# An attention kernel whose exponentials write eight fixed buffers in turn, with the order between them and the maxima declared away

## The chip, the cores and the metric

The kernel runs on one core of a Trainium2 chip. The metric is the device time of one execution in microseconds; the time before is the median of three runs, 921.76 us. The core has five engines with queues of their own: TensorE (PE, whose weight loads are listed as PEld), VectorE (DVE), ScalarE (ACT), GpSimd (POOL) and SyncE (SP, which here starts the DMAs). They meet only at semaphores: an instruction may wait until another engine's counter has reached a value, and its queue stands still behind it until then.

## The reference

Two attentions over the same x (2048 x 448, 16 heads of 28), mixed by a gate for each row:

```python
x = A_x
g = _sigmoid((x * gate_w).sum(-1, keepdims=True))
a = _A_ref(x, A_wqkv, A_wo)
b = _B_ref(x, B_wqkv, B_wo)
return g * a + (1 - g) * b
...
scores = jnp.einsum("bhqd,bhkd->bhqk", q, k) * (Dh ** -0.5)
p = _softmax(scores, axis=-1)
o = jnp.einsum("bhqk,bhkd->bhqd", p, v)
```

A is local: each position looks at eight positions, two apart, back from itself. B, of which the last three lines are the core, is full softmax attention. The output is float32.

## The kernel before, in words

The kernel has three stages. Up to some 260 us it projects x to the queries, keys and values of both attentions. Each number is split there into a high and a low part of a faster matmul format, and a product is summed from three products of parts. From 261 us on runs the main loop of B, and behind it, from about 845 us, the output projection.

The main loop has 256 steps: 16 units u (four groups g of four heads, by four blocks b of 512 queries), and in each unit 16 blocks kt of 128 keys. The softmax of a unit needs the maximum of each row ahead of its exponentials, so there are two passes. The first pass computes plain scores in high parts only (`s1_mm`, L142, 1024 matmuls in all) and takes maxima over 512 keys (`s1_max`, L146). The first 320 of these tiles are done among the projections; the other 704 are spread over the main loop, three to a step, for units that come later. So 235 steps carry first-pass work and the last 21 don't. The second pass computes the scores of the present unit (`scores`, L959: three matmuls a head, the terms QH·KH, QL·KH and QH·KL, with the negative maximum riding in two extra rows of QH), then the exponential (L962), and one step later the product with the values (`do_av`, L925).

The order of every engine's queue is the order of the code (`manual_schedule`); the framework only places the semaphore waits. A step's order on PE is written out as a list of tokens:

```python
WITH = "10 20 s0 11 21 30 00 12 22 31 01 s1 s2 32 02".split()
```

A token of two digits is a score matmul: the first digit is the head in the step's rotation, the second the term. `s0`, `s1` and `s2` are the first-pass matmuls. Heads 1 and 2 fill the two banks of the PSUM pair `one`; behind token 22 ACT turns both into probabilities with one exponential, the first of the step. Heads 3 and 0 fill the pair `mine`; behind 02 comes the second. Token s0 fills the single bank T1, read by a maximum of 128 x 512 (the T1 maximum). s1 and s2 fill the third pair, `other`, read by one maximum of 128 x 1024 (the pair maximum). After each step `mine` and `other` change places. So tokens 30 and 00 write banks that the pair maximum of the step before has read, and s1 and s2 write banks that the second exponential of the step before has read. Last on PE in each step come the four AV matmuls of the step before (each has two records in the trace).

An exponential writes a probability tile of 128 x 1024 from the pool `pp`, which has eight slots; each exponential asks for a new tile, `pair("P")`. The AV matmuls read it a step later.

Besides this, DVE and POOL compute attention A during the steps up to about 760 us: POOL multiplies queries by shifted keys (L599), folds 40 of the 64 products to half their length (L604), and DVE sums them in 176 small sums (L609); POOL then multiplies by the values and adds up (L649, L654). A list with costs and due steps sets behind which step each of these instructions stands. DVE has the T1 maximum, the pair maximum and then the small sums in each step; ACT has the two exponentials and now and then a copy.

Where an instruction needs more than one semaphore, the framework puts the further waits into separate EVENT_SEMAPHORE instructions ahead of it on its queue; a view of the trace by line lists them under DVEq and ACTq.

Of the kernel before, what the change touches and what calls it, by code (L numbers as in the profile page):

```python
# [10 lines left out]
AF = mybir.ActivationFunctionType  # L11
ALU = mybir.AluOpType
X = mybir.AxisListType.X
# [6 lines left out]
SCALE = DH ** -0.5  # L20
NU = NG * NB
NMX = 192
# [3 lines left out]
def gated_mix_kernel(ctx: ExitStack, tc: tile.TileContext, xT, xn, gw, wA, wB, woAB, out):  # L26
    nc = tc.nc
# [45 lines left out]
    MX = cp.tile([128, NMX], F32, name="MX")  # L73
# [10 lines left out]
    def pair(name):  # L84
        return pp.tile([128, 2, 512], F32, tag="P", name=name)
# [50 lines left out]
    def s1_mm(n, bank, half=False):  # L136
        u, i = divmod(n, 64)
        qs, kc, h = i // 16, i // 4 % 4, i % 4
        if i == 0 and u + 1 < NU:
            load_qhi(u + 1)  # L140
        r = slice(64 * (h // 2), 64 * (h // 2) + 64) if half else slice(32 * h, 32 * h + DH)
        nc.tensor.matmul(bank, qhis[u][h % 2][r, 128 * qs:128 * qs + 128],  # L142
                         KH[u // NB % 3][r, 512 * kc:512 * kc + 512], start=True, stop=True)

    def s1_max(n, k, bank):
        nc.vector.tensor_reduce(MX[:, n % NMX:n % NMX + k], bank, axis=X, op=ALU.max)  # L146
        if n // 64 != (n + k) // 64:
            finished.append(n // 64)
        s1c[0] = n + k
# [53 lines left out]
    with tc.tile_pool(name="xp", bufs=1) as xp, tc.tile_pool(name="wp", bufs=2) as wp:  # L203
# [208 lines left out]
        for kt in range(3):  # L412
            if kt < 2:
                nc.vector.tensor_copy(xh[0][:, kt, :], r[:, kt, :])
            nc.vector.tensor_tensor(out=xl[0][:, kt, :], in0=r[:, kt, :], in1=xh[0][:, kt, :].bitcast(F32),
                                    op=ALU.subtract)
        nc.vector.tensor_tensor(out=tail[64:128], in0=t[64:128], in1=tail[64:128].bitcast(F32), op=ALU.subtract)
        nc.vector.tensor_tensor(out=wl0[:, 3, 0:256], in0=wt0[:, 0:256], in1=wh0[:, 3, 0:256].bitcast(F32),
                                op=ALU.subtract)
# [27 lines left out]
        for n, t in enumerate(tiles):  # L447
# [4 lines left out]
            for w in splits:  # L452
                i, k = (n - splits[w][0]) * splits[w][1], splits[w][1]
# [42 lines left out]
            if n == 64:  # L496
                gate = []
                for sgn, dst in ((-1.0, g_t), (1.0, omg)):
                    e = sp.tile([128, NJ], F32, name="ez")
# [174 lines left out]
    for c in range(8):  # L674
# [20 lines left out]
        n = 0  # L695
# [240 lines left out]
    def scores(u, kt, cur):  # L936
        g = u // NB
        n = s1c[0]
        k = min(3, s1e - n)
        qh, ql = Qs[u]  # L940
        ks = slice(128 * kt, 128 * kt + 128)
        one, mine, other = ring
        ring[:] = (one, other, mine) if k else (other, one, mine)
        bank = {"1": one[:, 0, :], "2": one[:, 1, :], "3": mine[:, 0, :], "0": mine[:, 1, :],
                "s0": T1, "s1": other[:, 0, :], "s2": other[:, 1, :]}
        for tok in WITH if k else ALONE:
            if tok[0] == "s":
                i = int(tok[1])
                if i < k:
                    s1_mm(n + i, bank[tok])  # L950
                if i == 0:
                    s1_max(n, 1, T1)
                elif i == 2 and k > 1:
                    s1_max(n + 1, k - 1, other[:, 0:k - 1, :])
                continue
            a, t = tok[0], int(tok[1])
            h = (int(a) + n) % 4
            r = slice(32 * h, 32 * h + (DH + 2 if t == 0 else DH))
            nc.tensor.matmul(bank[a], (KH[g % 3], KH[g % 3], KL[g % 2])[t][r, ks], (qh, ql, qh)[t][r, :], start=(t == 0), stop=(t == 2))  # L959
            if t == 2 and a in "20":  # L960
                p = pair("P")
                nc.scalar.activation(p, one if a == "2" else mine, AF.Exp, scale=SCALE)  # L962
                cur[(h + 3) % 4], cur[h] = p[:, 0, :], p[:, 1, :]
                yield len(cur)

    for u in range(NU):
        g, b = divmod(u, NB)
        for kt in range(NJ):
# [12 lines left out]
            for a in scores(u, kt, cur):  # L981
                if a == 2:
                    run("mid", st)
# [66 lines left out]
```

## Time and profile before

| | |
|---|---|
| times of three runs | 921.76, 920.22, 921.76 us |
| span of the profiled execution | 921.0 us |
| main loop, steps with first-pass work | 261 to 794 us |
| main loop, steps without it | 794 to about 845 us |
| DVE busy in 350 to 700 us | 331.19 us |
| POOL busy in 350 to 700 us | 342.62 us |
| granted clock, 261 to 794 us | 1.00 |

A row of the groups reads: line, engine, operation, what it writes and reads with partitions x elements, how often, then busy time and mean duration in ns, then the idle time of the engine just before them and what ended it. A row of the order in time reads: start and length in us, engine, line, operation, and in brackets the idle time before. Neighbouring instructions of one group are merged in one row, so "x2" is two of them in one stretch. The ends of matmuls are modelled.

### The profile page before, as it was taken

The page shows a single profiled execution, that of the slowest core. Times are in us where ns is not written, and L with a number is a line of the kernel's source. Part 1 is how long each engine was busy: PE and PEld are TensorE (multiplying, and loading weights), DVE is VectorE, ACT ScalarE, POOL GpSimd, SP SyncE. Part 2 cuts the span into 40 slices and gives each one's busy share as a digit, 9 for nine tenths or more (in the row PEclk, how much of TensorE's full clock was granted, in tenths as well). Part 3 has the DMA queues.
Part 4 walks back from the last instruction along what each step waited for, and adds up shares of the span by engine and source line. Part 5 has one row for each costly group of instructions (what it writes and reads, how often), then busy time and mean ns, then how long its engine had stood idle before and what let it go on. Part 6 is the DMA issues. An engine that isn't in the chain of part 4 may idle for free.

```text
span 921.0 us, 21402 instructions
## 1 busy us (share of the span) xinstructions
PE 911.3 (99%) x8390; PEld 547.3 (59%) x8390; DVE 731.6 (79%) x975; ACT 649.8 (71%) x797; POOL 624.0 (68%) x488
## 2 busy tenths in 40 slices
PE   8999999999999999999999999999999999999998
PEld 6799999998944444444444444444444444335997
DVE  6488999998979999999999999999998888501221
ACT  6456434343378888888888888888989889996221
POOL 2389846464469799999999999999994851300100
PEclk9999999999999999999999999999999999999999
DMA  9877503559462342235135232431312123441572
GB/s 264 276 247 193 158 12 82 142 132 97 116 241 64 101 121 51 84 105 129 41 94 157 83 102 61 132 84 26 106 47 53 33 50 100 135 132 51 158 218 87
DMA packets 103966, 105.11 MB, mean 114 GB/s; under 512 B 64136, under 2 KB 73736, under 8 KB 103080
## 3 DMA queue, kind: packets, MB, share of 16 engines
q1 hardware_dynamic: 103720, 103.47, 41.5%
q8 instruction: 66, 1.08, 0.5%
q10 hardware_dynamic: 144, 0.26, 0.1%
q14 instruction: 36, 0.29, 0.1%
HBM read 62.72 MB, written 40.96 MB: 113 GB/s over the span
## 4 chain that ended last, share of the span: by engine, by line
PE 96%; DMA 2%; DVE 1%; ACT 1%; issue 0%; SPq 0%; ACTq 0%; DVEq 0%
PE T L959 31%; PE av L925 27%; PE r L295 15%; PE T L803 7%; PE r L290 6%; PE r L142 4%; PE T L142 4%; DMA V<-in_xT 1%; PE T L781 1%; DMA KH<-qk_hi 0%; DMA qk_hi<-qkh 0%; ACT P L962 0%; DVE xl L212 0%; SPq L99 0%; DVE MX L159 0%
## 5 line engine op out<-in xcount | busy, mean ns | idle before, releaser
L962 ACT ACTIVATE P<-T 128x1024 f32<-128x1024 f32 x512 | 497.0, 1024 | 66.0 <-PE T L959 64.9
L146 DVE TENSOR_REDUCE MX<-T 128x1 f32<-128x512 f32 x470 | 443.4, 954 | 39.2 <-PE T L959 16.4
L925 PE MATMUL av<-P,V 128*32 128x512 f32 x2048 | 272.7, 605 | 0.4 <-ACT osb L821 0.4
L959 PEld LDWEIGHTS T<-QH,KH 30*128 30x128 f32 x1024 | 92.5, 181 | 238.4 <-ACT P L962 197.5
L959 PE MATMUL T<-QH,KH 30*128 30x512 f32 x1024 | 222.9, 492 | 0.2 <-ACT P L962 0.2
L142 PE MATMUL T<-KH,QP 28*128 28x512 f32 x704 | 222.6, 463 | 0.1
L159 DVE TENSOR_REDUCE MX<-r 128x2 f32<-128x1024 f32 x160 | 192.1, 1222 | 27.1 <-PE r L142 23.4
L959 PE MATMUL T<-QH,KL 28*128 28x512 f32 x1024 | 190.8, 391 | 0.0
L959 PE MATMUL T<-QL,KH 28*128 28x512 f32 x1024 | 190.2, 392 | 0.0
L599 POOL TENSOR_TENSOR prod<-qt,kt 128x896 f32<-128x896 f32 x64 | 135.1, 2115 | 4.8 <-DMA kt<-a_scr 4.8
L358 ACT ACTIVATE raw<-r 128x896 f32<-128x896 f32 (+1 forms) x64 | 58.9, 921 | 99.4 <-PE r L295 93.7
L654 POOL TENSOR_TENSOR oat<-oat,prod 128x896 f32<-128x896 f32 x56 | 118.2, 2110 | 2.4
L142 PEld LDWEIGHTS T<-KH,QP 28*128 28x128 f32 x704 | 86.0, 181 | 23.2 <-ACT P L962 10.2
L359 POOL TENSOR_TENSOR ast<-raw 128x448 f32<-128x448 f32 x48 | 55.5, 1155 | 60.3 <-ACT raw L358 50.6
L649 POOL TENSOR_TENSOR prod<-vt,L 128x896 f32<-128x896 f32 x56 | 95.4, 1704 | 0.6
L959 PEld LDWEIGHTS T<-QH,KL 28*128 28x128 f32 x1024 | 93.5, 183 | 0.7
L959 PEld LDWEIGHTS T<-QL,KH 28*128 28x128 f32 x1024 | 93.4, 184 | 0.0
L925 PEld LDWEIGHTS av<-P,V 128*32 128x32 f32 x2048 | 40.3, 108 | 79.9 <-issue 66.8
L295 PE MATMUL r<-wh,xh 64*128 64x448 f32 (+1 forms) x512 | 82.8, 363 | 0.3 <-ACT raw L358 0.3
L142 PE MATMUL r<-KH,QP 64*128 64x512 f32 x320 | 80.5, 394 | 2.0 <-DMA KH<-qk_hi 0.8
L295 PE MATMUL r<-wh,xl 64*128 64x448 f32 (+1 forms) x384 | 70.4, 364 | 0.0
L295 PEld LDWEIGHTS r<-wh,xh 64*128 64x128 f32 x512 | 63.2, 185 | 1.5 <-ACT raw L358 0.6
(101 smaller groups left out, 1049.9 us busy)
## 6 DMA issues: line engine op xcount, KB each, us to landing
a_scr<-ast SPq DMA_DIRECT2D x24, 448.0 KB
qk_hi<-qkh SPq DMA_DIRECT2D x24, 256.0 KB
qk_lo<-qkh SPq DMA_DIRECT2D x24, 256.0 KB
rbc<-rs SPq DMA_DIRECT2D x64, 64.0 KB
QP<-qk_hi SPq DMA_DIRECT2D x64, 56.0 KB
KL<-qk_lo SPq DMA_DIRECT2D x16, 224.0 KB
QH<-qk_hi SPq DMA_DIRECT2D x64, 56.0 KB
QL<-qk_lo SPq DMA_DIRECT2D x64, 56.0 KB
```

Of the source, the lines that this page charges most:

```text
L142: nc.tensor.matmul(bank, qhis[u][h % 2][r, 128 * qs:128 * qs + 128], KH[u // NB % 3][r, 512 * kc:512 * kc + 512], start=True, stop=True)
L146: nc.vector.tensor_reduce(MX[:, n % NMX:n % NMX + k], bank, axis=X, op=ALU.max)
L159: nc.vector.tensor_reduce(m, PM[k], axis=X, op=ALU.max)
L295: nc.tensor.matmul(bank[:, 0:cols], x, ws[c][rows, k, 0:cols], start=first, stop=last)
L358: nc.scalar.activation(raw[:, :, 0:cols], PJ[n % 2][:, :, 0:cols], AF.Copy)
L599: nc.gpsimd.tensor_tensor(out=p, in0=qt[c], in1=kvt["k", c % 2][:, HALO - DIL * w:HALO - DIL * w + NJ, :], op=ALU.mult)
L649: nc.gpsimd.tensor_tensor(out=dst.rearrange("p j (h d) -> p j h d", d=DH), in0=kvt["v", c % 2][:, HALO - DIL * w:HALO - DIL * w + NJ, :].r ...
L654: nc.gpsimd.tensor_tensor(out=oat[c], in0=oat[c], in1=oat[c, w], op=ALU.add)
L803: writes(bank, nc.tensor.matmul(bank[:, :D], src, wo[c][:, k, :], start=(first and k == ks[0] and i == 0), stop=(last and k == ks[-1] and ...
L925: nc.tensor.matmul(av[32 * h:32 * h + 32, :], V[:, kt, 4 * g + h, :], tiles_[h], start=(kt == 0), stop=(kt == NJ - 1), skip_group_check=True)
L959: nc.tensor.matmul(bank[a], (KH[g % 3], KH[g % 3], KL[g % 2])[t][r, ks], (qh, ql, qh)[t][r, :], start=(t == 0), stop=(t == 2))
L962: nc.scalar.activation(p, one if a == "2" else mine, AF.Exp, scale=SCALE)
```

## The change

Two things change, both in the main loop. The first eight exponentials take a probability tile from the pool and keep it in a list; every later one writes the tile of eight exponentials before instead of asking for a new one. And edges are declared to the framework as needing no wait: from a maximum to the last eight exponentials; from an exponential to the one that wrote its buffer before; and from an exponential to the last four maxima. The reasons given in the code are that PE waited for the one named and the instruction at hand waits for PE. The waits for PE stay. No instruction that computes is added, removed or moved; the 176 small sums and the 40 folds are as they were.

```diff
+    exps, maxs, probs = [], [], []
+
     def s1_max(n, k, bank):
-        nc.vector.tensor_reduce(MX[:, n % NMX:n % NMX + k], bank, axis=X, op=ALU.max)
+        i = nc.vector.tensor_reduce(MX[:, n % NMX:n % NMX + k], bank, axis=X, op=ALU.max)
+        for e in exps[-8:]:
+            tc.declare_no_dep(i.ins, e, reason="PE waited for it and the maximum waits for PE")
+        maxs.append(i.ins)
         if n // 64 != (n + k) // 64:
             finished.append(n // 64)
         s1c[0] = n + k
...
             if t == 2 and a in "20":
-                p = pair("P")
-                nc.scalar.activation(p, one if a == "2" else mine, AF.Exp, scale=SCALE)
+                if len(exps) < 8:
+                    probs.append(pair("P"))
+                p = probs[len(exps) % 8]
+                e = nc.scalar.activation(p, one if a == "2" else mine, AF.Exp, scale=SCALE).ins
+                for o in exps[-8:-7]:
+                    tc.declare_no_dep(e, o, query=mybir.DependencyQuery.ANY_SYNC,
+                                      reason="PE has read what it wrote, and this one waits for PE")
+                for o in maxs[-4:]:
+                    tc.declare_no_dep(e, o, reason="PE waited for it and the exponential waits for PE")
+                exps.append(e)
                 cur[(h + 3) % 4], cur[h] = p[:, 0, :], p[:, 1, :]
                 yield len(cur)
```

## The prediction

> **What bounds the kernel now.** I read the page first, then the busy time by stretch, the groups by form and the waits inside the main loop, and last a few steps in order of time.
>
> ```profile
> span 921.0 us, 21402 instructions
> PE 911.3 (99%) x8390; PEld 547.3 (59%) x8390; DVE 731.6 (79%) x975; ACT 649.8 (71%) x797; POOL 624.0 (68%) x488
> ...
> PE 96%; DMA 2%; DVE 1%; ACT 1%; issue 0%; SPq 0%; ACTq 0%; DVEq 0%
> ```
> ```profile
> 261.00:794.00 533.00, 532.78 (x5354) 220.51 (x5346) 496.22 (x717) 469.14 (x530) 462.51 (x323) 1.00 0.34 91
> 350.00:700.00 350.00, 349.78 (x3516) 144.73 (x3512) 331.19 (x499) 307.12 (x347) 342.62 (x229) 1.00 0.33 86
> ```
>
> Columns of the second view: stretch, length, busy time of PE, PEld, DVE, ACT, POOL, granted clock, DMA share, GB/s. Everything the diff touches runs between 261 and 794 us, the steps that mix second-pass scores with first-pass maxima. PE looks full there, the chain of work that ended last is 96% PE and the clock is whole, so removing waits on ACT and DVE would seem to buy nothing. But matmuls on different row groups overlap, and a busy PE need not be at its peak. DVE is busy for 496.2/533 = 93%, ACT for 88%.
>
> ```profile
> L962 ACT ACTIVATE P<-T 128x1024 f32<-128x1024 f32 x466 | 452.5, 1024 | 63.9 <-PE T L959 62.8
> L146 DVE TENSOR_REDUCE MX<-T 128x2 f32<-128x1024 f32 x233 | 285.0, 1223 | 19.8 <-PE T L959 11.1 <-PE T L142 0.2
> L925 PE MATMUL av<-P,V 128*32 128x512 f32 x1864 | 248.2, 605 | 0.0
> L609 DVE TENSOR_REDUCE L<-prod 128x8 f32<-128x224 f32 x96 | 33.7, 371 | 0.0
> ```
>
> Eight AV records make a step: 1864/8 = 233 steps in 533 us, 2.29 us each. Now three of them.
>
> ```profile
> 500.83 0.50 PE L959 MATMUL T<-QH,KH 30*128 30x512 f32 x2
> ...
> 501.40 2.01 DVE L146 TENSOR_REDUCE MX<-T 128x1 f32<-128x512 f32 x2
> ...
> 501.64 0.42 PE L142 MATMUL T<-KH,QP 28*128 28x512 f32 x2
> ...
> 501.90 1.94 ACT L962 ACTIVATE P<-T 128x1024 f32<-128x1024 f32 x2 [0.39 <-PE T L959]
> 502.13 1.06 PE L925 MATMUL av<-P,V 128*32 128x512 f32 x8
> 503.13 0.49 PE L959 MATMUL T<-QH,KH 30*128 30x512 f32 x2
> ...
> 503.47 0.50 PE L959 MATMUL T<-QH,KH 30*128 30x512 f32 x2
> ...
> 503.70 0.39 PE L959 MATMUL T<-QH,KL 28*128 28x512 f32 x2
> ...
> 504.20 1.94 ACT L962 ACTIVATE P<-T 128x1024 f32<-128x1024 f32 x2
> 504.37 1.06 PE L925 MATMUL av<-P,V 128*32 128x512 f32 x8
> 505.36 0.50 PE L959 MATMUL T<-QH,KH 30*128 30x512 f32 x2
> ...
> 506.19 0.49 PE L142 MATMUL T<-KH,QP 28*128 28x512 f32 x2
> ...
> 506.80 1.23 DVE L146 TENSOR_REDUCE MX<-T 128x2 f32<-128x1024 f32 x1 [0.16 <-PE T L959]
> ...
> 508.06 0.64 DVE L609 TENSOR_REDUCE L<-prod 128x16 f32<-128x224 f32 x2
> 508.08 0.50 PE L959 MATMUL T<-QH,KH 30*128 30x512 f32 x2
> ...
> 508.62 1.81 DVE L146 TENSOR_REDUCE MX<-T 128x1 f32<-128x512 f32 x2
> ...
> 509.97 0.50 PE L959 MATMUL T<-QH,KH 30*128 30x512 f32 x2
> ...
> 510.48 0.50 PE L959 MATMUL T<-QH,KH 30*128 30x512 f32 x2
> ...
> 512.36 0.50 PE L959 MATMUL T<-QH,KH 30*128 30x512 f32 x2
> ```
>
> Columns: start and length in us. A step opens with QH,KH of tokens 10 and 20 (500.83, 503.13, 505.36). The opening waits for no exponential: it comes 1.00 us after the AV group's start at 502.13 and 0.99 after that at 504.37, although the first exponential of the pair (1.02 us each) ended 0.21 us before the one opening and 0.14 before the other. It is PE's own pace.
>
> The second QH,KH pair, tokens 30 and 00, is different. At 503.47 it follows the end of the pair maximum (501.40 + 2.01 = 503.41) by 0.06; at 508.08 it follows 506.80 + 1.23 = 508.03 by 0.05; at 510.48 it follows 508.62 + 1.81 = 510.43 by 0.05. That maximum reads the bank pair into which these matmuls write. So 30/00 come 0.34 us after the opening at 503.13 but 0.51 after that at 509.97, and the next opening comes 1.89, 1.89 and 1.88 us after the three: the delay goes through to the step. PE, busy or not, runs at the pace of loops through DVE and ACT. Three kinds show here.
>
> *Loop A*, two steps: opening 500.83, first-pass matmuls s1/s2 501.64, pair maximum until 503.41, 30/00 503.47, opening 505.36. 4.53 us, 2.27 a step, one pair maximum that waited for PE.
> *Loop B*, three steps: opening 503.13, exponentials 504.20 to 506.14, s1/s2 0.05 later at 506.19 (they write what the second exponential read), pair maximum 506.80 to 508.03, 30/00 508.08, opening 509.97. 6.84 us, 2.28 a step, one exponential and one pair maximum that waited for PE.
> *Chained DVE*: where DVE has no gap (508.06 local sums, 508.62 both maxima, until 510.43), a loop gains one step in which nothing waits for PE: B becomes 503.13 to 512.36, 9.23 us over four, 2.31 a step.
>
> **The change, part by part.** *Fixed buffers.* The pool already holds eight slots and nothing else takes them in this loop, so the same eight buffers come round in the same order: no memory, copy or DMA is added, and the price is nothing. The three lists are made in Python and issue nothing.
>
> *Waits removed.*
>
> ```profile
> L962 ACT ACTIVATE P<-T x175: 1017/1024/1049, 499.6 to 699.2; 128x1024 f32<-128x1024 f32 x175
> L962 ACTq EVENT_SEMAPHORE  x173: 17/17/17, 501.8 to 699.5; - x173
> L146 DVE TENSOR_REDUCE MX<-T x176: 624/952/1227, 499.4 to 699.6; 128x1 f32<-128x512 f32 x88, 128x2 f32<-128x1024 f32 x88
> L146 DVEq EVENT_SEMAPHORE  x87: 21/21/21, 502.1 to 699.5; - x87
> ```
>
> Almost every exponential has a separate wait ahead of it, and of the maxima one kind does: 87 waits for 88 pair maxima. An instruction holds one wait itself; a second becomes an instruction of its own. The declared edges leave each with PE alone, so the separate instructions should go: some 233 on DVE and 466 to 512 on ACT. Most of them stand ahead of an instruction that queues behind its own engine anyway (the second exponential; the maxima in the 1.81 us pair at 508.62, shorter than 0.69 + 1.23 on their own) and are worth nothing, as the running instruction covers them. Where the engine idles until PE is done, the wait is on the path. Its price is how much later the work starts than with PE's wait inside the instruction:
>
> ```profile
> L146 DVEq EVENT_SEMAPHORE  x1: 21/21/21, 548.0 to 548.0; - x1
> 548.02 1.23 DVE L146 TENSOR_REDUCE MX<-T 128x2 f32<-128x1024 f32 x1 [0.19 <-PE T L959]
> L962 ACTq EVENT_SEMAPHORE  x2: 17/17/17, 568.2 to 568.3; - x2
> 568.31 1.02 ACT L962 ACTIVATE P<-T 128x1024 f32<-128x1024 f32 x1 [0.38 <-PE T L959]
> 516.87 0.49 PE L142 MATMUL T<-KH,QP 28*128 28x512 f32 x1
> 517.44 0.69 DVE L146 TENSOR_REDUCE MX<-T 128x1 f32<-128x512 f32 x1 [0.17 <-PE T L142]
> ```
>
> A wait shown at 548.0 ended no earlier than 547.95, and its maximum began at 548.02: at most 0.07 between. One shown at 568.2 was no later than 568.25, its exponential began at 568.31: at least 0.06. From below: a T1 maximum, whose only wait is in the instruction, starts 517.44 − (516.87 + 0.49) = 0.08 us after the modelled end of its matmul, the pair maximum 506.80 − (506.19 + 0.49) = 0.12 after, the exponential 504.20 − (503.70 + 0.39) = 0.11 after: 0.03 to 0.04. So the bounds are 0.03 and 0.07. I take 0.065 for DVE and 0.06 for ACT, because the wait's own record is nearer to the thing than a modelled end.
>
> By the Trainium skill, "VectorE: DVE Perf Modes", section "The DRAIN you can't avoid", a semaphore after each of a chain of DVE operations cost nothing extra over one at the end. That would make this edit worth zero; the rows agree where DVE queues behind itself, and not where it idles until PE.
>
> *The sum.* Loop A saves 0.065 in two steps, 0.033 a step; loop B 0.125 in three, 0.042; with a chained step these become 0.022 and 0.031. Over 233 steps: 7.6, 9.7, 5.1 and 7.3 us. Following the releases back from the last such step to the first, as above, I count 69 loops, 51 of them through an exponential: 69 × 0.065 + 51 × 0.06 = 7.5 us. That is the most this chain can give, since others almost as long take over as it shrinks. I take the middle between it and the lowest loop: (7.5 + 5.1)/2 = 6.3 us. With prices of 0.03 for both it would be 3.6 on the same chain, with 0.07 for both 8.4.
>
> *Late next.* PE's own pace: the step opened at 503.13 lasted 2.23 us, still under 2.29 − 0.03 = 2.26. And POOL: 342.6 of 350 us busy leaves 7.4 us, 0.048 a step over 153 steps, above the 0.027 I use.
>
> Span: 921.0 − 6.3 = 914.7. The median shown is 0.8 above this span; 921.8 − 6.3 = 915.5 us.
>
> **The rivals.** *POOL takes over.* If its 7.4 us are gaps it cannot close, the 153 steps keep their pace and only 80 gain, 80 × 0.027 to 0.042 = 2.2 to 3.4 us: 918.4 to 919.6. For it: the 98%. Against: the local sums, which need POOL's products, show 0.0 us of idle before them.
>
> *Nothing to gain.* The waits are free, or the framework puts others in their place (the exponential's wait for the AV matmuls that read its buffer, say, which is PE's too and should fold into the one kept): 921.8. Against the first: the 0.06 above.
>
> *The loops go altogether*, all steps at 2.23 us: 233 × 0.06 = 14 us, 908. It needs DVE to stop queueing at 93% busy.
>
> *Slower.* Telling the framework less makes other instructions wait for themselves. The dear place is PE ahead of its AV group: if fixed buffers make it wait for the exponentials separately, at 0.06 (ACT's price) on the engine that closes every loop, 233 steps cost 14.0 us, less 6.3 is 7.7: 929.5. From 6.3/0.06 = 105 such waits on, the kernel is slower.
>
> ```profile
> PEld T L959 <- ACT P L962: 194.8, 232, 1.1
> PEld av L925 <- issue: 65.8, 219, 0.4
> ```
>
> Against it: the opening weight loads already carry a wait for the exponential, 232 times; the AV group comes later on the same queue, and its idle time shows no release by ACT P now.
>
> **How the numbers follow.** A difference under 0.2% (1.84 us) can't be told from no change. Forecast, with any mix of the loops (5.1 to 9.7 saved, 912 to 916.7): 0.60. POOL or another chain keeps part of it (1.9 to 5.1 saved): 0.16. Loops go further than 9.7: 0.07. Nothing: 0.11. Slower: 0.06. Faster is 0.60 + 0.16 + 0.07 = 0.83. The range 910.5 to 920.3 takes in both prices of the wait and leaves out nothing gained, slower, and the far part of the large gain, 0.20 in all.
>
> **What would show it.** The separate waits of L962 and L146 fall from about one per exponential and per pair maximum to a handful. An exponential that idled starts about 0.05 us, not 0.11, after its matmul's modelled end; a pair maximum 0.06, not 0.12. 30/00 still follow the pair maximum by 0.05, now nearer to the opening, and the stretch of 233 steps shrinks from 533 to about 527 us. Before 261 us and after 794 nothing moves. A shorter lag with the same step would say the loops are not the bound; a wait of POOL's ahead of the local sums would be the first rival; idle before the AV loads released by ACT P, the last.

## The result, and the profile after

The changed kernel takes 913.08 us (912.09 to 914.14), the kernel before 921.76. The ratio is 0.9913, 95% interval 0.9896 to 0.9929: between 6.5 and 9.6 us faster, where 6.3 was forecast. In a later set of runs the same pair gave 0.9920 (0.9907 to 0.9932).

The page after, its busy line and its chain:

```profile
span 910.4 us, 20673 instructions
PE 901.8 (99%) x8390; PEld 545.7 (60%) x8390; DVE 730.6 (80%) x975; ACT 649.1 (71%) x797; POOL 623.1 (68%) x488
...
PE 72%; POOL 20%; DMA 4%; SPq 1%; issue 1%; DVE 1%; ACT 1%; POOLq 0%; ACTq 0%
```

There are 21402 − 20673 = 729 instructions fewer, and no computing one among them: the counts behind the five engines are as before. What is gone shows in the views by line, 500 to 700 us, which before listed 173 and 87 separate waits:

```profile
L969 ACT ACTIVATE P<-T x177: 1003/1023/1046, 499.8 to 699.5; 128x1024 f32<-128x1024 f32 x177
L148 DVE TENSOR_REDUCE MX<-T x178: 630/950/1227, 499.4 to 699.9; 128x1 f32<-128x512 f32 x89, 128x2 f32<-128x1024 f32 x89
```

Neither line lists an EVENT_SEMAPHORE now. (L969 is L962 of before, L148 is L146, L964 is L959, L930 is L925.) The groups of the main loop:

```profile
L969 ACT ACTIVATE P<-T 128x1024 f32<-128x1024 f32 x465 | 451.7, 1025 | 56.5 <-PE T L964 55.4
L148 DVE TENSOR_REDUCE MX<-T 128x2 f32<-128x1024 f32 x232 | 283.6, 1222 | 8.0 <-PE T L964 1.3 <-PE T L142 0.2
L148 DVE TENSOR_REDUCE MX<-T 128x1 f32<-128x512 f32 x233 | 160.1, 687 | 22.3 <-PE T L142 13.1 <-PE T L964 6.8
```

The durations are the same; the idle time ahead of the pair maxima fell from 19.8 to 8.0 us, that ahead of the exponentials from 63.9 to 56.5. That ahead of the T1 maxima rose from 16.7 to 22.3. Some rows in order of time show the lags:

```profile
501.12 0.50 PE L964 MATMUL T<-QH,KH 30*128 30x512 f32 x2
...
501.49 0.50 PE L964 MATMUL T<-QH,KH 30*128 30x512 f32 x2
...
501.69 0.39 PE L964 MATMUL T<-QH,KL 28*128 28x512 f32 x2
...
502.02 1.81 DVE L148 TENSOR_REDUCE MX<-T 128x1 f32<-128x512 f32 x2
...
502.13 1.94 ACT L969 ACTIVATE P<-T 128x1024 f32<-128x1024 f32 x2 [0.38 <-PE T L964]
...
503.37 0.50 PE L964 MATMUL T<-QH,KH 30*128 30x512 f32 x2
```
```profile
558.33 0.50 PE L142 MATMUL T<-KH,QP 28*128 28x512 f32 x2
558.87 1.23 DVE L148 TENSOR_REDUCE MX<-T 128x2 f32<-128x1024 f32 x1
```

The exponential starts 502.13 − (501.69 + 0.39) = 0.05 us after the modelled end of its matmul, where 0.11 was read before. The pair maximum starts 558.87 − (558.33 + 0.50) = 0.04 after, where it was 0.12. The rows are typical: over the steps with first-pass work, the median lag of the first exponential fell from 0.104 to 0.043 us, that of the pair maximum from 0.113 to 0.044. Tokens 30/00 come 0.37 us after this opening, and the next opening 1.88 us after them, as before.

To see where the time came from, each execution is cut at three records of the AV matmuls: the first, the first of the 234th group and the first of the last (256th) group. That gives four parts: what is ahead of the loop, the 233 steps, the 22 up to the last AV group, and the tail.

| profiled execution | ahead | 233 steps | last steps | tail | span |
|---|---|---|---|---|---|
| before | 261.5 | 533.9 | 47.0 | 78.5 | 921.0 |
| before, again | 262.0 | 534.1 | 47.0 | 78.6 | 921.6 |
| after | 258.2 | 527.2 | 46.4 | 78.6 | 910.4 |
| after, again | 259.3 | 527.2 | 46.5 | 78.6 | 911.4 |

The part ahead holds no edited line, and its differences look like chance: it varies between 258.2 and 262.0 us over the kernels of this study, whether they have the change or not. The 233 steps repeat to 0.1 us. So the change is worth 533.94 − 527.23 = 6.7 us there and 0.5 us in the last steps, 7.2 together; the 8.7 between the two medians probably holds some of that chance besides, and 7.2 lies within both intervals.

### The profile page after: what moved, and what is told of

Same layout as the page of the kernel before. It is cut to its first block, busy times and chain, and to the rows that moved or that the text cites. A ratio compares the mean times of both kernels' runs of the same rounds, so it can differ in the third digit from the quotient of the medians.

```text
span 910.4 us, 20673 instructions
## 1 busy us (share of the span) xinstructions
PE 901.8 (99%) x8390; PEld 545.7 (60%) x8390; DVE 730.6 (80%) x975; ACT 649.1 (71%) x797; POOL 623.1 (68%) x488
## 3 DMA queue, kind: packets, MB, share of 16 engines
q8 instruction: 66, 1.08, 0.5%
## 4 chain that ended last, share of the span: by engine, by line
PE 72%; POOL 20%; DMA 4%; SPq 1%; issue 1%; DVE 1%; ACT 1%; POOLq 0%; ACTq 0%
PE T L964 19%; PE av L930 17%; PE r L300 15%; PE T L808 8%; PE r L295 6%; POOL oat L659 6%; POOL prod L604 5%; POOL prod L654 5%; PE r L142 4%; PE T L142 3%; DMA V<-in_xT 1%; POOL prod L609 1%; DMA oa_scr<-oat 1%; POOL on L855 1%; SPq L99 1%
## 5 line engine op out<-in xcount | busy, mean ns | idle before, releaser
L969 ACT ACTIVATE P<-T 128x1024 f32<-128x1024 f32 x512 | 496.9, 1025 | 58.2 <-PE T L964 56.3
L148 DVE TENSOR_REDUCE MX<-T 128x1 f32<-128x512 f32 x470 | 441.5, 954 | 33.1 <-PE T L142 15.7
L930 PE MATMUL av<-P,V 128*32 128x512 f32 x2048 | 272.8, 605 | 0.4 <-ACT osb L826 0.4
L964 PEld LDWEIGHTS T<-QH,KH 30*128 30x128 f32 x1024 | 92.6, 182 | 231.5 <-ACT P L969 199.0
L142 PE MATMUL T<-KH,QP 28*128 28x512 f32 x704 | 220.3, 456 | 0.1
L964 PE MATMUL T<-QH,KH 30*128 30x512 f32 x1024 | 213.0, 490 | 1.8 <-ACT P L969 1.1
L964 PE MATMUL T<-QH,KL 28*128 28x512 f32 x1024 | 187.0, 395 | 0.0
L964 PE MATMUL T<-QL,KH 28*128 28x512 f32 x1024 | 185.1, 393 | 0.0
L964 PEld LDWEIGHTS T<-QL,KH 28*128 28x128 f32 x1024 | 94.1, 185 | 0.0
L964 PEld LDWEIGHTS T<-QH,KL 28*128 28x128 f32 x1024 | 93.6, 183 | 0.6
L930 PEld LDWEIGHTS av<-P,V 128*32 128x32 f32 x2048 | 40.5, 108 | 78.0 <-issue 65.1
```

What stands on the lines that cost most here:

```text
L148: i = nc.vector.tensor_reduce(MX[:, n % NMX:n % NMX + k], bank, axis=X, op=ALU.max)
L930: nc.tensor.matmul(av[32 * h:32 * h + 32, :], V[:, kt, 4 * g + h, :], tiles_[h], start=(kt == 0), stop=(kt == NJ - 1), skip_group_check=True)
L969: e = nc.scalar.activation(p, one if a == "2" else mine, AF.Exp, scale=SCALE).ins
```

## The experiments

Each was compared with runs of the kernel before on the same chip. "Steps" are the 233 steps of its profile, cut as above. The diffs are against the changed kernel.

**The parts of the change, one at a time.** First the unchanged kernel for its stages:

> The kernel before once more, unchanged, for its stages. The 233 steps took 534 us before and 527 after, and the projections ahead of them 261.5 and 258.2 us, though the diff doesn't touch them. If those 3.4 us are chance, this run may show projections anywhere near 258 to 262 us, with 233 steps of 534 us again. If the change itself shortened the projections, they take 261 to 262 us here and 258 in every kernel that has the change.

Steps 534.1 us; ahead of them 262.0. Then only the maxima:

```diff
-                if len(exps) < 8:
-                    probs.append(pair("P"))
-                p = probs[len(exps) % 8]
+                p = pair("P")
...
-                for o in exps[-8:-7]:
...
-                for o in maxs[-4:]:
```

> Only the maxima lose their waits for exponentials; the exponentials are as before, with new buffers from the pool. Loops theory: each of the 69 loops has one pair maximum that waits for PE, 69 x 0.065 = 4.5 us at most, some 3.8 expected; 233 steps of 530 us, about 918 us. Rival (ACT alone carries the gain, the maxima queue behind DVE anyway): 921.8 us, 233 steps of 534.

917.2 us, ratio 0.9958 (0.9942 to 0.9974), steps 529.5: 4.5 less. Only the exponentials:

```diff
-        for e in exps[-8:]:
-            tc.declare_no_dep(i.ins, e, reason="PE waited for it and the maximum waits for PE")
```

> Only the exponentials change (fixed buffers, no waits for maxima and for themselves); the maxima keep their separate wait. Loops theory: 51 of the 69 loops pass through an exponential that waits for PE, 51 x 0.06 = 3.1 us at most, some 2.6 expected; 233 steps of 531.4 us, about 919.2 us. Rival (ACT alone): the whole gain, about 913 us. Rival (maxima alone): 921.8 us.

917.1 us, 0.9952 (0.9939 to 0.9964), steps 530.3: 3.6 less, and 46.5 in the last steps, where the maxima alone gave 47.3. Then the buffers, with no declared edge:

> The eight fixed buffers with no edge declared away: every separate wait is there as before. Loops theory: no difference, 921.8 us within 0.2%, 233 steps of 534 us. Rival (the buffers themselves save something, for instance in what the pool's release costs): up to the 8.7 us of the change, 913 us.

921.7 us, 0.9999 (0.9990 to 1.0008), steps 534.2. The buffers by themselves do nothing. The views by line, 500 to 700 us, show which wait each variant kept; first the one with the maxima alone, then the one with the exponentials alone:

```profile
L967 ACTq EVENT_SEMAPHORE  x175: 17/17/411, 500.7 to 698.4; - x175
```
```profile
L148 DVEq EVENT_SEMAPHORE  x88: 21/21/21, 500.5 to 698.8; - x88
```

Both kinds of wait pay, and neither rival that gave all to one of them holds.

**Which of the exponentials' waits.** Two complements, both with fixed buffers and the maxima left alone: one loses only the wait for itself, the other only the waits for maxima.

```diff
-                for o in maxs[-4:]:
-                    tc.declare_no_dep(e, o, reason="PE waited for it and the exponential waits for PE")
```

> As in the run with the exponentials alone, but only the wait for themselves is declared away, so the second exponential of each step keeps a separate wait for a maximum and the first one has none. Loops theory: the second one queues behind the first anyway, so its separate wait is free: the same 917.1 us as with both declared (233 steps 530.3 us). Rival (every separate wait costs): half the gain, about 919.3 us.

917.6 us, 0.9951 (0.9939 to 0.9964), steps 530.1. The view by line of this kernel, 500 to 700 us:

```profile
L967 ACT ACTIVATE P<-T x176: 1015/1023/1060, 499.7 to 699.3; 128x1024 f32<-128x1024 f32 x176
L967 ACTq EVENT_SEMAPHORE  x83: 17/17/17, 503.3 to 699.3; - x83
```

83 waits for 176 exponentials: half of them kept one, and the gain is the same as with none.

```diff
-                for o in exps[-8:-7]:
-                    tc.declare_no_dep(e, o, query=mybir.DependencyQuery.ANY_SYNC,
-                                      reason="PE has read what it wrote, and this one waits for PE")
```

> The complement: fixed buffers, only the exponentials' waits for maxima declared away, the wait for themselves kept, so that PE's wait stands in a separate instruction ahead of every exponential. Loops theory: nothing, 921.7 us within 0.2%, 233 steps 534 us. Rival (every separate wait costs): some 2 us faster.

921.9 us, 0.9997 (0.9989 to 1.0006), steps 534.1. The records of the trace say which semaphore stands where. In the kernel before and in this one, an exponential that finds ACT idle has the wait for PE in the separate instruction and the wait for ACT itself in its own; with the wait for itself gone it holds PE's wait alone, and nearly all separate waits that are left belong to exponentials that queue behind ACT and wait for DVE. So the exponentials' gain comes from the first of each step, where the wait for PE moved into the instruction; the second queues behind it and its separate wait costs nothing. Two of the three sets of edges do the work: those of the maxima, and that of an exponential to the writer of its buffer. (No run has these two sets and not the third.)

**Is POOL the next bound?** After the change the page puts 20% of its chain on POOL.

```diff
-            nc.gpsimd.tensor_tensor(out=oat[c], in0=oat[c], in1=oat[c, w], op=ALU.add)
+            if w % 2 == 0:
+                nc.gpsimd.tensor_tensor(out=oat[c], in0=oat[c], in1=oat[c, w], op=ALU.add)
```

> The changed kernel with 32 of POOL's 56 additions of local attention left out (those of odd shifts; the local attention is then incomplete): 32 x 2.11 = 68 us less on POOL. Loops theory: POOL is not the bound, 913.1 us within 0.2%, 233 steps 527 us. Rival (POOL is the new bound after the change, its share of the chain being 20% on the page): several us faster, 233 steps under 524 us.

913.7 us, 0.9907 (0.9893 to 0.9920): no different from the change in its time, in which 261.6 us ahead of the loop hide it, but the steps took 525.3 us, 1.9 less than with the change. The trace says where. The changed kernel at a unit's end, in order of time:

```profile
614.38 1.31 POOL L855 TENSOR_TENSOR on<-osb,rbc 128x512 f32<-128x512 f32 x1
...
615.73 0.63 ACT L859 ACTIVATE onhi<-on 128x512 fp32r<-128x512 f32 x1 [1.08 <-POOL on L855]
...
616.27 1.92 ACT L969 ACTIVATE P<-T 128x1024 f32<-128x1024 f32 x2
...
617.33 0.50 PE L964 MATMUL T<-QH,KH 30*128 30x512 f32 x2 [1.11 <-ACT P L969]
```

And the kernel before at the same place:

```profile
620.33 1.29 POOL L850 TENSOR_TENSOR on<-osb,rbc 128x512 f32<-128x512 f32 x1
...
622.86 0.63 ACT L854 ACTIVATE onhi<-on 128x512 fp32r<-128x512 f32 x1
623.38 1.94 ACT L962 ACTIVATE P<-T 128x1024 f32<-128x1024 f32 x2
```

Before, POOL ended its product at 621.62 and ACT reached the copy that needs it 1.24 us later. With shorter steps ACT reaches it first, waits 1.08 us at the head of its queue, the exponentials behind it are late, and now the opening does wait for an exponential. The waits of PE in the loop of the changed kernel:

```profile
PE T L964 <- ACT P L969: 1.1, 1, 1.1
PE T L964 <- DMA QH<-nm: 0.6, 1, 0.6
```

They sum to 1.7 us, at two openings of new units; before it was 0.2 us, and with less on POOL the view is empty. The second row is the other place, and there POOL seems to act through SyncE: SyncE's queue stood 8.7 us for another product of POOL (L840), and behind it stand the loads for the next unit, on the last of which the opening waited. POOL is a bound in two places of 233, not in the loop at large.

**Are the chained steps the rest?** The changed kernel with short small sums:

```diff
-        nc.vector.tensor_reduce(..., prods[c, w][:, r], axis=X, op=ALU.add)
+        nc.vector.tensor_reduce(..., prods[c, w][:, r, 0:2], axis=X, op=ALU.add)
```

> The changed kernel with each of the 176 small sums reading 2 elements of a row in place of 14 or 28 (the local scores are then incomplete): each some 0.25 us shorter, 44 us less on DVE. Loops theory: the chained steps vanish, what is left are loops A at (4.53 - 0.065)/2 = 2.23 and B at (6.84 - 0.125)/3 = 2.24 us a step: 233 steps of 520 to 522 us against 527, some 6 us faster, 907 us. Rival (PE's own pace now sets the step): no change, 913 us.

914.4 us, 0.9917 (0.9902 to 0.9933), steps 526.9: a miss. The sums were indeed short, by the groups of DVE in its main loop:

```profile
L148 DVE TENSOR_REDUCE MX<-T 128x1 f32<-128x512 f32 x466 | 444.1, 956 | 52.5 <-PE T L142 26.2 <-PE T L964 9.3
L614 DVE TENSOR_REDUCE L<-prod 128x16 f32<-128x32 f32 (+1 forms) x176 | 24.6, 163 | 0.0
```

DVE gained 37 us and spent it waiting for PE. Part of the expected gain went into the same two openings, where PE now lost more:

```profile
PE T L964 <- ACT P L969: 1.6, 1, 1.6
PE T L964 <- DMA QH<-nm: 1.4, 1, 1.4
```

Without them the steps are 523.9 against 525.5 for the change, 1.6 us for the 37.

The releases can be followed back through this trace as in the prediction, a matmul being counted as held where it starts within 0.08 us of the end that it waits for. Of 70 loops, 46 are then of kind B without chained DVE, at 2.240 us a step: the 2.24 that was expected. Of the rest, 13 take four steps and have one of ACT's copies in the queue with the exponentials, at 2.26 to 2.27 us a step but for the one with the late opening. Chained DVE stands in 6 loops, where the changed kernel has it in 35 of 64. So the chained steps did go, but most of the chained loops had taken only 2.25 to 2.26 us a step in the changed kernel, little above B's 2.24, and there was little to gain.

Two more runs tried ACT's copies (the first with the short sums as well):

```diff
-        nc.scalar.activation(t, av, AF.Copy)
+        if u < NU - 1:
+            nc.vector.tensor_copy(t, av)
...
-        nc.scalar.activation(fin["hi"], fin["on"], AF.Copy)
+        if u < NU - 1:
+            nc.vector.tensor_copy(fin["hi"], fin["on"])
...
```

> The kernel with short small sums (local scores incomplete, as there) and with ACT's two larger copies of each unit, 0.6 us each, moved to DVE, which has room there. That kernel kept 2.26 us a step although the loops A and B, with the durations measured in it, give 2.22 to 2.24. Theory (ACT's copies stretch the loops that pass through the exponentials): steps of 2.24 us or less, 233 steps about 521 us against 527, time about 908 us. Rival (something else, PE's own pace for one): 527 us again, 914 us.

921.0 us, 0.9997 (0.9988 to 1.0006), steps 534.8.

> The same move of ACT's two copies to DVE in the changed kernel with its sums whole. DVE gains 1.2 us in 16 steps and ACT loses it. If ACT's copies are on the loops more often than DVE has a queue: some us faster, 908 to 912 us. If DVE's queue pays as much as ACT saves: 913 us or slower.

926.8 us, 1.0055 (1.0039 to 1.0071), steps 538.1. Both are slower than their counterparts by 8 and 11 us of steps. They don't show what the copies cost on ACT, because the move is no exchange of equals: the copy that rounds took 0.63 us on ACT and, in the first of the two kernels,

```profile
L863 DVE CAST onhi<-on 128x512 fp32r<-128x512 f32 x13 | 15.2, 1168 | 0.0
```

1.17 us on DVE, ahead of a T1 maximum (1.01 us in the second). PE now waited for maxima, 4.9 us in the first kernel and 4.6 in the second, where with the change alone it waited for none. In the last steps, where DVE has little to do, both kernels were faster: 45.5 and 45.8 us, against 46.4.

**Another order on PE.** The changed kernel with

```diff
-    WITH = "10 20 s0 11 21 30 00 12 22 31 01 s1 s2 32 02".split()
+    WITH = "10 20 s0 11 21 30 00 12 22 s1 s2 31 01 32 02".split()
```

> The changed kernel with s1 and s2 issued ahead of 31 and 01 on PE. Loops theory: the pair maximum's matmuls come up to 0.06 us earlier where they don't wait for an exponential, 69 loops x 0.06 = 4 us faster, about 909 us. Rival: in the 80 steps in which s1 waits for the second exponential of the step before, 31 and 01 now wait behind it, 0.1 to 0.15 us each: no gain or up to 8 us slower, 913 to 921 us.

931.1 us, 1.0105 (1.0090 to 1.0119), steps 544.2: slower than either case foresaw. Rows in order of time:

```profile
501.82 0.50 PE L964 MATMUL T<-QH,KH 30*128 30x512 f32 x2
...
502.47 0.50 PE L964 MATMUL T<-QL,KH 28*128 28x512 f32 x2
502.62 0.40 PE L142 MATMUL T<-KH,QP 28*128 28x512 f32 x2
502.81 0.40 PE L964 MATMUL T<-QH,KL 28*128 28x512 f32 x2
...
503.13 1.06 PE L930 MATMUL av<-P,V 128*32 128x512 f32 x8
```

s1/s2 come 0.80 us after the opening, as in the older order (501.64 − 500.83 = 0.81 in the kernel before), although their place in the list is two tokens earlier: PE's own pace puts them there. Only the last scores move back, and AV with them, here 1.31 us after the opening; the mean is 1.34, against 1.26 in the changed kernel. In none of 230 steps do 30/00 start within 0.08 us of the end of a pair maximum, or s1/s2 of an exponential. Here PE is the bound, at 2.34 us. Why this order takes it longer was not tested.

**The change once more**, for the part ahead of the loop:

> The changed kernel once more, unchanged, on the same chip as the next ones. The main loop's 233 steps 527 us again; the projections ahead of it, which the diff doesn't touch, took 258.2 us in its first profile and 258.6 to 262.0 in the other kernels: if they are shorter because of the change they take 258 again, if that was chance anything from 258 to 262. Time 913 us, 8 to 9 us below the kernel before.

914.2 us, 0.9920 (0.9907 to 0.9932), steps 527.2, ahead 259.3. The variant above with 534.1 us of steps had 258.6 ahead, the one with less on POOL 261.6 with 525.3: the part ahead goes its own way.

## Why the prediction was right

*The bound.* Held. PE's busy time hid a loop through DVE and ACT; taking 0.06 to 0.07 us from waits on those engines shortened the whole, with PE's work unchanged. The opening still paid no heed to the exponentials, except at two unit boundaries.

*Fixed buffers cost and bring nothing.* Held: 0.9999 of the time, 534.2 us of steps. In the code the edge to the earlier writer is declared between exponentials on one fixed buffer; no run tried it with buffers from the pool.

*Waits where an engine queues behind itself are free.* Held, by the pair of runs that kept one half or the other.

*The price of a wait.* 0.06 us was right for the exponential, whose median lag fell from 0.104 to 0.043. 0.065 for the pair maximum was slightly low: from 0.113 to 0.044, 0.07. The bounds 0.06 and 0.07 that the prediction read off the wait's own records run from where such a record starts, not from where it ends, 0.02 us later.

*The sum.* This is the step that was mis-sized. 7.5 us was called the most the chain could give, and 6.3 taken because other chains would take over. But the parts gave 4.5 and 3.6 us where that count gave at most 4.5 and 3.1, and together 533.94 − 525.26 = 8.7 us where POOL is relieved. So little was lost to other chains; a likely reason is that nearly every loop of the kind passes through a pair maximum, so that all shrink together. With the prices measured, the count gives 69 × 0.07 + 51 × 0.06 = 7.9. The rest may lie in the count, which depends on which of two releases close together is taken: counted again on the same trace, in two ways, it gives 44 and 53 exponentials in place of 51. POOL then took back 1.9 of the 8.7. The 6.7 us that are left in the steps agree with 6.3 in part because two errors, a gain too small and POOL's share left out, cancel.

*Late next.* POOL was named for its lack of spare time, as a cap of 0.048 us on each step. It acted otherwise: not a step at a time, but through two late products, one that stood ahead of the exponentials on ACT's queue and one ahead of the next unit's loads on SyncE's.

*After 794 us nothing moves.* Wrong by 0.5 us: the first exponential's wait was on the path in the last steps too. The kernels that lost it took 46.4 to 46.5 us there (45.5 and 45.8 with the copies moved as well), those that kept it 47.0, or 47.3 with the maxima alone changed.

*Span and time.* The 0.8 us put between span and median was wrong: in the changed kernel an execution of 912.18 us has a span of 910.4, so by the same 1.8 us the profiled execution of before took some 922.8 us; the slowest on record is 922.86. The forecast was taken off the median, so it didn't suffer.

*The rivals.* The free wait holds only where an instruction queues behind its own engine: a T1 maximum and a pair maximum back to back take 1.81 us with a separate wait for the second (508.62 in the kernel before) and without one (502.02 in the changed kernel). The Trainium skill, "VectorE: DVE Perf Modes", section "The DRAIN you can't avoid", states from eight copies in a row that a semaphore after each DVE operation costs nothing extra over one after the last. There the trace agrees; ahead of an idle DVE it does not, by the 0.07 us above. The slower case, with waits turning up on PE, did not come: the count of all instructions fell by just the 729, and the AV groups start 1.26 us after the opening (501.12 to 502.38), no later than before (1.30, 500.83 to 502.13).

## What to carry to other kernels

An engine that is 99% busy can still be paced by a loop through other engines: look for a matmul that always starts the same few hundredths after another engine's instruction ends, and check whether a delay of it reaches the next step. On such a loop a second semaphore ahead of an instruction cost 0.06 to 0.07 us here each time the engine had been idle, and nothing when it queued behind itself; so it pays to find which declared edge folds the last wait into the instruction, and to leave the others. When steps shorten, look at the head of each queue for an instruction that needs a slower engine's product: its spare time can shrink with the steps (at the place shown, from 1.24 us to none).

## What the runs showed of the hardware

A copy of 128 x 512 from float32 into the matmul format of the split parts (fp32r in the rows) took 0.63 us on ACT, and 1.17 or 1.01 us on DVE in the two kernels that moved it. And a large wait in a row was not one on the path:

```profile
PEld T L964 <- ACT P L969: 196.3, 232, 2.0
```

Before the change it was 194.8 us in 232 waits, so it stood through a gain of 7 us. The weight load is put down as held by that semaphore, but the opening came 0.99 to 1.00 us after the AV group's start whether the exponential had ended 0.14 or 0.21 us ahead of it.
